# An attention block: earlier first tiles, projections released one by one, 280 instead of 252 VectorE score tiles, and another closing chain

## The chip, the cores and the metric

The kernel runs on one core of a Trainium2 chip. The metric is the time of one execution in microseconds of device time. Before the change it is 402.87 us, the median of three runs (402.79 to 403.15).

## The reference

One multi-head self-attention block in bfloat16: 2048 tokens (S), width 448 (D), 16 heads of 28 (Dh).

```python
B, S, D, H = 1, 2048, 448, 16          # x ~ 0.05 N(0,1), wqkv and wo too
qkv = (x @ wqkv).reshape(B, S, 3, H, Dh).transpose(2, 0, 3, 1, 4)
q, k, v = qkv[0], qkv[1], qkv[2]
scores = jnp.einsum("bhqd,bhkd->bhqk", q, k) * (Dh ** -0.5)
p = softmax(scores, axis=-1)
o = jnp.einsum("bhqk,bhkd->bhqd", p, v)
return o.transpose(0, 2, 1, 3).reshape(B, S, D) @ wo
```

## The kernel before

**Tiling.** Four heads make a group g (G = 4 groups), 512 queries make a chunk c (4 chunks). A *unit* u is one group with one chunk, so there are 16 units, worked through in the order u = 4g + c. In a unit the keys come in 16 blocks of 128 (kt), and each block gives four *tiles*, one per head: 128 keys by 512 queries of scores. There are 16 x 16 x 4 = 1024 tiles. TensorE makes the scores of a tile (matmul at L704), something turns them into exponentials, and TensorE multiplies these with V into one PSUM bank, ACC (L656), where all 16 key blocks of a unit add up. A column of ones in V gives the softmax sums in the same pass.

**Two ways to exponentials.** Most tiles go through ScalarE (L741): groups of three and two tiles in turn, each group one instruction, out to the slots of PT. The key blocks that `d_kts` names go through VectorE instead. For such a block (a *batch*, four tiles) VectorE first makes an integer from each score tile (L759, called R below, PSUM to PD), then three shifted copies of all four tiles (L766, called H, three instructions of 2048 elements). Read as bfloat16, these four rows of PD, each weighted by a copy of V that is scaled (VC, made by GpSimd at L465 from VX), add up to an approximated exponential. So a VectorE batch costs four passes of four PV matmuls where a ScalarE block costs one. Before, unit 0 has 3 batches and every other unit 4: 63 batches, 252 tiles; 772 tiles go to ScalarE.

**Projections.** `proj_qk` (L430) and `proj_v` (L450) make Q, K and V of one group and chunk, a *job* of 16 matmuls in one PSUM bank of the pool M (banks 5 and 6), which the scores of the VectorE tiles use too. VectorE copies a job's bank out (L410, L412, and VX at L459). Group 0's K and V stand at the front; the other 39 jobs carry priorities from L485.

**End of a unit.** `post_unit` copies ACC out (L593, ACCEV), sends the sums through DRAM and back in another layout (scr_l, LT), takes their reciprocal (L615), spreads it over partitions through DRAM (scr_r, RB), and GpSimd multiplies (L638) into OTN. When group 3 is done for a chunk, `out_proj` multiplies with wo (L570), VectorE copies (L582) and SyncE stores (L584). For the last unit the reciprocal goes through TensorE (L603, L625) and VectorE (L630) instead of DRAM. At the very end a flag says whether all reciprocals lie in a safe range (L780 to L790); every engine waits for it, and a slower general version would follow if it were 0.

**What sets the order.** The program is recorded first (`P.add` with engine, dependences, a planned duration `dur` and a priority) and then planned by `_Prog.schedule`: at each step the engine that can start first takes, among what is ready within 150 ns, the instruction with the lowest `prio`. The result is one fixed list per engine. The score matmuls have priorities about -1000, so they go as soon as their PSUM banks are free; projections fill in by priority.

**Loads.** SyncE loads x transposed, in four chunks (L349, L351), then wo (L385). ScalarE's queue loads wqkv in three parts K, Q, V of 448 columns (L357, L359). Nine rounds of four matmuls on zeros (L393) stand ahead of TensorE's first projection.

Of the kernel before, what the change touches and what calls it, by code (L numbers as in the profile page):

```python
# [7 lines left out]
ALU = mybir.AluOpType  # L8
# [251 lines left out]
NTERM = 4  # L260
ZBIAS = 127.0 * 128.0 - 7.235034912313908


def _fast(nc, x, wqkv, wo, out, n_heads=16):
# [16 lines left out]
    NPT = 30  # L281
    NZ = 3
    NOB = 4
    scale = float(DH) ** -0.5
# [12 lines left out]
    with es:  # L297
# [9 lines left out]
        VC = sb("VC", [128, NCH, NTERM, HC], BF16)  # L307
        VX = sb("VX", [128, 4, GD], FP32)
# [4 lines left out]
        OTN = sb("OTN", [128, G, S], BF16)  # L313
# [3 lines left out]
        SEL = sb("SEL", [128, 4], FP32)  # L317
        CK1 = sb("CK1", [128, NU * 16], FP32)
        CK2 = sb("CK2", [128, NU * 16], FP32)
        CKM = sb("CKM", [128, 1], BF16)  # L320
# [24 lines left out]
        dma_x = []  # L345
        for c in range(NCH):
# [6 lines left out]
        dma_w = {}  # L353
        wv_ = wqkv[0:(NIT - 1) * KT_, :].rearrange("(it p) c -> p it c", p=KT_)
        for t, prio in ((1, -20), (0, -19), (2, -18)):
            grp = _DmaGroup(f"w{t}")
            P.add("act", (lambda e, t=t: e.dma_start(w_raw[:, 0:NIT - 1, t * D:(t + 1) * D], wv_[:, :, t * D:(t + 1) * D])),  # L357
                  dur=600, prio=prio, name=f"dma_w{t}a", dma_group=grp, nbytes=(NIT - 1) * KT_ * D * 2)
            dma_w[t] = P.add("act", (lambda e, t=t: e.dma_start(w_raw[KT_ - KTAIL:KT_, NIT - 1, t * D:(t + 1) * D],  # L359
                                                                wqkv[(NIT - 1) * KT_:D, t * D:(t + 1) * D])),  # L360
                             dur=600, prio=prio + 0.5, name=f"dma_w{t}b", dma_group=grp, nbytes=KTAIL * D * 2)
# [6 lines left out]
                       deps=[id_f_op], dur=100, prio=-6, name="sel")  # L368
        V4 = V.rearrange("p n (hh r) -> p (n hh) r", r=32)
# [11 lines left out]
        for g in range(G):  # L381
            for h in range(4):
                r0 = (4 * g + h) * DH
                p0 = 32 * h
                dma_wo.append(P.add("sp", (lambda e, g=g, r0=r0, p0=p0: e.dma_start(wop[p0:p0 + DH, g, :], wo[r0:r0 + DH, :])),  # L385
                                    deps=[ms_wop], after=dma_wo[-1:] + dma_x[-1:], dur=500, prio=-5, name=f"dma_wo{g}{h}", dma_group=grp_wo))

        warm_last = None
        for i in range(9):
# [1124 lines left out]
```

## Time and profile before

| | |
|---|---|
| median of three runs | 402.87 us |
| the profiled execution's own time | 401.62 us |
| its span, first to last instruction | 398.0 us |
| mean granted TensorE clock | 0.927 |
| HBM read and written | 5.66 MB and 2.08 MB |

The page of the profile gives for each engine the time in which it was busy. The views used below are: the busy time by stretches of the span, groups of instructions by line, the timeline of one stretch, the table of waits, and the DMA queues. An instruction's duration in these views is from its start to its end; where instructions of one engine follow each other closely, the next starts a little ahead of the end of the last, so that the distance from start to start is shorter than the duration. That distance is called the *step* below.

### The profile page before, as it was taken

To read this page: it belongs to the slowest core of one execution; us is meant where nothing else is said; L and a number is where in the kernel's file an instruction comes from. 1 tells how busy PE (TensorE), PEld (TensorE's weight loads), DVE (VectorE), ACT (ScalarE), POOL (GpSimd) and SP (SyncE) were. 2 spreads that over 40 slices of the span, in tenths; PEclk is the share of its full clock that TensorE was granted. 3 is DMA by queue.
4 is the path that set the end of the run, shared out by engine and by line. 5 is a ranking of instruction groups with operands and counts; after the bars stand their busy time and mean duration, and the time that the engine had idled before them with its cause. 6 is when DMAs were issued, how large, how long until landed. Compare 5 with 4: busy or idle time off the path is not lost.

```text
span 398.0 us, 8639 instructions
## 1 busy us (share of the span) xinstructions
PE 348.9 (88%) x3713; PEld 106.6 (27%) x3713; DVE 334.0 (84%) x557; ACT 357.0 (90%) x314; POOL 48.5 (12%) x97
## 2 busy tenths in 40 slices
PE   4999999999999999999798887868887779889784
PEld 1333323323333233333221111211122112222141
DVE  0488999999999989999988788887788899999651
ACT  1599999999999999999999999999899999999811
POOL 6121121111112011312001010010101010010100
PEclk9899999999999999999968687898689999999886
DMA  9900010100000000101000000100001011001011
GB/s 216 133 12 2 12 37 1 32 0 24 8 17 16 4 28 3 29 1 31 2 16 15 3 27 3 29 0 18 13 4 29 2 29 36 19 23 51 26 49 53
DMA packets 20230, 10.47 MB, mean 26 GB/s; under 512 B 14364, under 2 KB 18204, under 8 KB 20184
## 3 DMA queue, kind: packets, MB, share of 16 engines
q1 hardware_dynamic: 18744, 8.64, 9.0%
q10 hardware_dynamic: 1440, 1.20, 1.2%
q8 instruction: 30, 0.49, 0.5%
q14 instruction: 16, 0.13, 0.1%
HBM read 5.66 MB, written 2.08 MB: 19 GB/s over the span
## 4 chain that ended last, share of the span: by engine, by line
PE 43%; DVE 28%; ACT 24%; DMA 2%; issue 1%; SPq 0%
ACT PT L741 24%; PE ps L656 16%; PE ps L704 16%; DVE PD L759 12%; DVE PD L766 11%; PE ps L430 6%; PE ps L570 2%; PE ps L450 2%; DVE OTS L593 2%; DMA xT<-in_x_dram 2%; DVE QT L410 1%; DVE KT L412 1%; DVE V L412 1%; SPq L349 0%; PE ps L625 0%
## 5 line engine op out<-in xcount | busy, mean ns | idle before, releaser
L741 ACT ACTIVATE PT<-ps 128x1536 bf16<-128x1536 f32 (+1 forms) x309 | 353.8, 1292 | 12.1 <-PE ps L704 10.9
L759 DVE TENSOR_SCALAR PD<-ps 128x512 int16<-128x512 f32 x252 | 169.5, 685 | 31.3 <-PE ps L704 29.9
L704 PE MATMUL ps<-QT,KT 28*128 28x512 bf16 x1024 | 148.2, 407 | 22.6 <-ACT PT L741 19.3
L766 DVE TENSOR_SCALAR PD<-PD 128x2048 int16<-128x2048 int16 x189 | 131.2, 713 | 0.9
L656 PE MATMUL ps<-PD,VC 128*32 128x512 bf16 x1008 | 98.6, 416 | 11.9 <-DVE PD L766 7.9
L656 PE MATMUL ps<-PT,V 128*32 128x512 bf16 x772 | 76.5, 408 | 1.1 <-DVE OTS L593 1.1
L704 PEld LDWEIGHTS ps<-QT,KT 28*128 28x128 bf16 x1024 | 36.0, 91 | 141.8 <-ACT PT L741 96.2
L638 POOL TENSOR_TENSOR OTN<-RB,OTS 128x512 bf16<-128x512 f32 x15 | 20.3, 1355 | 199.9 <-DMA RB<-scr_r 199.8
L430 PE MATMUL ps<-xT,w_raw 128*32 128x512 bf16 x512 | 40.7, 397 | 4.4 <-DMA xT<-in_x_dram 4.0
L656 PEld LDWEIGHTS ps<-PD,VC 128*32 128x32 bf16 x1008 | 24.7, 96 | 54.2 <-DVE PD L766 26.8
L465 POOL TENSOR_SCALAR VC<-VX 128x112 bf16<-128x112 f32 x64 | 21.9, 342 | 124.8 <-DVE VX L459 121.8
L656 PEld LDWEIGHTS ps<-PT,V 128*32 128x32 bf16 x772 | 18.4, 94 | 41.2 <-issue 36.4
L450 PE MATMUL ps<-w_raw,xT 128*128 128x112 bf16 x256 | 19.2, 214 | 0.5 <-DVE QT L410 0.5
L570 PE MATMUL ps<-wop,OTN 128*128 128x448 bf16 x64 | 18.1, 415 | 0.8 <-DVE OTN L630 0.8
L430 PEld LDWEIGHTS ps<-xT,w_raw 128*32 128x32 bf16 x512 | 11.8, 98 | 22.0 <-issue 10.3
L582 DVE CAST OUTS<-ps 128x448 bf16<-128x448 f32 x14 | 8.7, 621 | 8.8 <-PE ps L570 8.6
L412 DVE CAST KT<-ps 128x512 bf16<-128x512 f32 x16 | 11.0, 685 | 6.1 <-PE ps L430 6.0
L450 PEld LDWEIGHTS ps<-w_raw,xT 128*128 128x128 bf16 x256 | 13.2, 98 | 10.6 <-issue 7.6
L580 ACT ACTIVATE OUTS<-ps 128x448 bf16<-128x448 f32 x2 | 1.1, 543 | 12.7 <-PE ps L570 12.7
L593 DVE COPY OTS<-ps 128x512 f32<-128x512 f32 x16 | 11.0, 685 | 0.7 <-PE ps L656 0.7
L410 DVE TENSOR_SCALAR QT<-ps 128x512 bf16<-128x512 f32 x15 | 10.3, 685 | 1.0 <-PE ps L430 0.8
L412 DVE CAST V<-ps 128x448 bf16<-128x448 f32 x16 | 9.9, 617 | 1.1 <-PE ps L450 1.1
(37 smaller groups left out, 35.9 us busy)
## 6 DMA issues: line engine op xcount, KB each, us to landing
RB<-scr_r SPq DMA_DIRECT2D x60, 64.0 KB, 2.0
out_dram<-OUTS SPq DMA_DIRECT2D x16, 112.0 KB, 1.7
w_raw<-in_wqkv_dram ACTq DMA_DIRECT2D x3, 336.0 KB, 5.5
wop<-in_wo_dram SPq DMA_DIRECT2D x16, 24.5 KB
scr_l<-OTS SPq DMA_DIRECT2D x15, 8.0 KB
LT<-scr_l SPq DMA_DIRECT2D x15, 8.0 KB, 1.5
scr_r<-RS SPq DMA_DIRECT2D x15, 8.0 KB, 1.4
w_raw<-in_wqkv_dram ACTq DMA_DIRECT2D x3, 56.0 KB, 5.3
```

Of the source, the lines that this page charges most:

```text
L412: fe = (lambda e: e.tensor_copy(evac[0](), evac[1](hold[0].banks[0])))
L430: ins = e.matmul(ps[32 * h:32 * h + 32, b * 512:(b + 1) * 512], w_raw[:, it, col:col + 32], xT[:, it, c * 512:(c + 1) * 512], start=(it == ...
L450: ins = e.matmul(ps[:, b * 512 + j * GD:b * 512 + (j + 1) * GD], xT[:, it, n * 128:(n + 1) * 128], w_raw[:, it, 2 * D + g * GD:2 * D + (g ...
L465: sc = P.add("pool", (lambda e, dst=dst, j=j: e.tensor_scalar(dst, src, TERM_C[j], 1.0, ALU.mult, ALU.mult)), deps=[ev2, ms_c1[j]], after= ...
L570: return e.matmul(bank(hold[0].banks[0])[:, 0:D], OTN[:, gg, n * 128:(n + 1) * 128], wop[:, gg, :], start=(gg == 0), stop=(gg == G - 1))
L593: accev = P.add("dve", (lambda e: e.tensor_copy(OTS[:, ub, :], bank(ACC))), deps=pv_ops[u] + [ots_last[ub]], dur=610, prio=-95.0, name=f"A ...
L638: nm = P.add("pool", (lambda e: e.tensor_tensor(OTN[:, g, c * QCH:(c + 1) * QCH], RB[:, ub, :], OTS[:, ub, :], ALU.mult)), deps=[l4], dur= ...
L656: return e.matmul(ps[32 * h:32 * h + 32, ACC * 512:(ACC + 1) * 512], lhsT, rhs, start=first, stop=False, skip_group_check=True, tile_posit ...
L704: return e.matmul(bank(b), KT[32 * h:32 * h + DH, g, kt * 128:(kt + 1) * 128], QT[32 * h:32 * h + DH, g, c * QCH:(c + 1) * QCH], start=Tru ...
L741: ex = P.add("act", (lambda e, p0=p0, w=w, b0=b0: e.activation(PT[:, p0 * 512:(p0 + w) * 512], bank(b0, w), AF.Exp, scale=ESCALE)), deps=[ ...
L759: r = P.add("dve", (lambda e, hold=hold, zs=zs, h=h: e.tensor_scalar(PD[:, zs, 0, h * 512:(h + 1) * 512], bank(hold[0].banks[0]), ZBIAS, 0 ...
L766: sh = P.add("dve", (lambda e, zs=zs, j=j: e.tensor_scalar(PD[:, zs, j, :], PD[:, zs, 0, :], float(TERM_D[j]), None, ALU.add)), deps=rs_ + ...
```

## The change

- **Loads.** ScalarE's queue now loads only columns 0 to 115 of K, Q and V each (head group 0 and four columns more). The other 332 columns of all three go on SyncE's queue, behind all of x and ahead of wo.
- **Zero matmuls ahead of the first projection**: 14 rounds of four instead of 9. In addition `pv_common` can append rounds on zeros to a PV round, in a number that `warm_fill` decides after planning from the planned times: it appends one where the plan has a gap of more than 278 ns behind a PV round and counts less than 56% of the last 3413 ns as work.
- **Projections.** Priorities run from 0.8 in steps of 0.28 (before: 0.7 and 0.25), and the first matmul of each of these jobs may not stand ahead of the score group whose position is 0.06 before its priority.
- **VectorE tiles.** Units 3, 5, 7, 9, 11 and 13 get a fifth batch (key block 13), unit 0 a fourth: 70 batches, 280 tiles; 744 tiles are left to ScalarE, in 298 instructions instead of 309. Of the shifted copies, the first is one instruction as before (L862 of the changed kernel), the second and third are one of 4096 elements (L864). VC gets five slots instead of four, VX two blocks per job. PT has 36 slots instead of 30.
- **End of a unit.** The products go into QT, whose chunk is no longer needed, instead of OTN. The reciprocal of a unit has priority -96 instead of about u + 1.
- **Closing.** A new function `tail` takes the place of the last unit's chain: the last chunk's output projection for groups 0 to 2 is made ahead (PREOP); ACC is copied in two halves; one fp32 matmul with a 0/1 matrix (SELB) spreads the sums over the partitions; the reciprocal is taken of 128x256 values and multiplied, per half; then one matmul per output tile adds group 3 (FINOP). The range check of units 0 to 14 is made ahead, and of the last unit alone behind.

```diff
 def d_kts(u):
-    if u == 0:
-        return (3, 7, 15)
+    if u in (3, 5, 7, 9, 11, 13):
+        return (3, 7, 11, 13, 15)
     return (3, 7, 11, 15)
...
-    pr = 0.7 + i / 4.0
+    pr = 0.8 + i * 0.28
...
+    while release and release[0][0] - 0.06 <= pos:
+        release.pop(0)[1].after.append(s)
...
-for i in range(9):
+for i in range(14):
...
+wk = load_w("act", 0, 2, 0, GD + 4, "wqk0", -20)
+dma_w[(2, 0)] = load_w("act", 2, 3, 0, GD + 4, "wv0", -19)
 for c in range(NCH):                     # x, as before, on SyncE's queue
...
+wr = load_w("sp", 0, 3, GD + 4, D, "wr", -6.2)
...
-for j in range(1, NTERM):
-    sh = P.add("dve", (lambda e, zs=zs, j=j: e.tensor_scalar(PD[:, zs, j, :], PD[:, zs, 0, :], float(TERM_D[j]), None, ALU.add)), ...)
+h1 = P.add("dve", (lambda e, zs=zs: e.tensor_scalar(PD[:, zs, 1, :], PD[:, zs, 0, :], float(TERM_D[1]), None, ALU.add)), ...)
+h2 = P.add("dve", (lambda e, zs=zs: e.tensor_scalar(PD[:, zs, 2:4, :], PD[:, zs, 0:2, :], float(TERM_D[2]), None, ALU.add)), ...)
...
+def tail():
+    for j in range(NQT):                 # PREOP: groups 0 to 2 of the last chunk
+            for gg in range(G - 1):
+                ins = e.matmul(bank(j)[:, 0:D], QT[:, gg, n * 128:(n + 1) * 128], wop[:, gg, :], start=(gg == 0), stop=False, ...)
+    for k in range(2):                   # ACC copied in halves
+        av.append(P.add("dve", (lambda e, cs=cs: e.tensor_copy(OTS[:, ub, cs], bank(ACC)[:, cs])), ...))
+    for k in range(2):
+        bc = P.add("pe", (lambda e, ...: e.matmul(bank(...)[:, 0:H2], SELB[:, :], OTS[:, ub, cs], start=True, stop=True)), ...)
+        rc = P.add("dve", (lambda e, ...: e.reciprocal(RB[:, ub, cs], bank(...)[:, 0:H2])), ...)
+        dv = P.add("dve", (lambda e, ...: e.tensor_tensor(QT[...], OTS[:, ub, cs], RB[:, ub, cs], ALU.mult)), ...)
+        for j in (2 * k, 2 * k + 1):     # FINOP: group 3, then copy out and store
```

**Where the program differs: the start.** On ScalarE's queue, the loads of the weights w_raw stand first. Before:

```order
L357 DMA w_raw<-in_wqkv_dram 128x3x448
L359 DMA w_raw<-in_wqkv_dram 64x448
L357 DMA w_raw<-in_wqkv_dram 128x3x448
L359 DMA w_raw<-in_wqkv_dram 64x448
L357 DMA w_raw<-in_wqkv_dram 128x3x448
L359 DMA w_raw<-in_wqkv_dram 64x448
```

Of the change, ScalarE's queue up to the first activation that reads loaded data (the copy of Q):

```order
L383 DMA w_raw<-in_wqkv_dram 128x3x116 x2
L385 DMA w_raw<-in_wqkv_dram 64x2x116
L383 DMA w_raw<-in_wqkv_dram 128x3x116
L385 DMA w_raw<-in_wqkv_dram 64x116
L371 ACT_TABLE_LOAD
L371 ACTIVATE WARM<-WARM 128x1
L455 ACTIVATE QT<-ps 128x512
```

The three parts of 448 columns became three of 116; the remaining 3 x 332 columns stand on SyncE's queue behind the eight transposing loads of x.

**The middle.** TensorE's list before, where its last projection stands (L430; L704 are scores, L656 PV rounds): 497 of the 1024 score matmuls are ahead of it, which is in unit 7.

```order
L704 MATMUL ps<-QT,KT 128x512 x2
L430 MATMUL ps<-xT,w_raw 32x512 x4
L704 MATMUL ps<-QT,KT 128x512
L656 MATMUL ps<-PD,VC 32x512 x4
L704 MATMUL ps<-QT,KT 128x512 x4
L656 MATMUL ps<-PT,V 32x512 x8
```

TensorE's list of the change, where its last projection stands (L477; L798 are scores, L750 PV rounds): 920 score matmuls are ahead of it, which is in unit 14.

```order
L477 MATMUL ps<-xT,w_raw 32x512 x8
L798 MATMUL ps<-QT,KT 128x512 x2
L477 MATMUL ps<-xT,w_raw 32x512 x8
L750 MATMUL ps<-PD,VC 32x512 x4
L798 MATMUL ps<-QT,KT 128x512 x5
L750 MATMUL ps<-PD,VC 32x512 x4
```

The projections moved from units 0 to 7 (208, 64, 84, 76, 88, 76, 92 and 80 matmuls) to units 0 to 14 (160, 56, 56, 56, 52, 20, 80, 16, 64, 16, 48, 16, 112, 0 and 16). In the whole list of the change the only matmuls on zeros (ZM, ZW) are the 56 of the 14 rounds at the start: behind no PV round does one stand.

**The end.** TensorE's list before, from its last scores on (L570 is the output projection, 16 matmuls for a chunk; L603 and L625 turn and spread the reciprocal):

```order
L704 MATMUL ps<-QT,KT 128x512 x2
L570 MATMUL ps<-wop,OTN 128x448 x16
L656 MATMUL ps<-PT,V 32x512 x8
L603 MATMUL ps<-SEL,OTS 128x4 x4
L625 MATMUL ps<-id_f,RS 32x128 x16
L570 MATMUL ps<-wop,OTN 128x448 x16
```

TensorE's list of the change, from its last scores to the spreading of the sums (L620 is the output projection of the chunk before, L684 PREOP, L698 the spreading matmul):

```order
L798 MATMUL ps<-QT,KT 128x512
L620 MATMUL ps<-wop,QT 128x448 x8
L750 MATMUL ps<-PD,VC 32x512 x8
L750 MATMUL ps<-PT,V 32x512 x12
L750 MATMUL ps<-PD,VC 32x512 x8
L620 MATMUL ps<-wop,QT 128x448 x16
L750 MATMUL ps<-PD,VC 32x512 x8
L750 MATMUL ps<-PT,V 32x512 x12
L750 MATMUL ps<-PD,VC 32x512 x16
L684 MATMUL ps<-wop,QT 128x448 x3
L698 MATMUL ps<-OTS,SELB 128x256 x2
```

Behind the last scores there now stand 64 PV matmuls and 24 of the output projection instead of 8 and 16. Behind L698 follow the four matmuls for the range check (L724) and then, in turn, FINOP and the other three PREOPs.

More of the change, by code (lines that the diff above doesn't have):

```diff
@@ L280, in _fast @@
     GD = 4 * DH
-    NPT = 30
+    NPT = 36
     NZ = 3
     NOB = 4
+    NDK = len(D_SLOT)
     scale = float(DH) ** -0.5
@@ L569, in f_op @@
                 def f_op(e, gg=gg):
-                    return e.matmul(bank(hold[0].banks[0])[:, 0:D], OTN[:, gg, n * 128:(n + 1) * 128], wop[:, gg, :],
+                    return e.matmul(bank(hold[0].banks[0])[:, 0:D], QT[:, gg, n * 128:(n + 1) * 128], wop[:, gg, :],
                                     start=(gg == 0), stop=(gg == G - 1))
```

235 lines of the change are left out of this document (161 added, 74 removed).

## The prediction, made before the change was run

> **What bounds the kernel now.** First the page, for the engines' shares, then busy time by stretches, to see whether one engine holds the end everywhere.
>
> ```profile
> span 398.0 us, 8639 instructions
> ...
> PE 348.9 (88%) x3713; PEld 106.6 (27%) x3713; DVE 334.0 (84%) x557; ACT 357.0 (90%) x314; POOL 48.5 (12%) x97
> ```
>
> ```profile
> core 0: us, PE busy (x) PEld busy (x) DVE busy (x) ACT busy (x) POOL busy (x), PEclk, DMA share, GB/s
> 30.00:200.00 170.00, 163.68 (x1940) 54.05 (x1941) 164.01 (x280) 166.34 (x147) 27.93 (x59) 1.00 0.05 14
> 200.00:300.00 100.00, 82.81 (x765) 19.19 (x757) 80.84 (x131) 94.81 (x83) 5.22 (x4) 0.80 0.05 13
> 300.00:330.00 30.00, 22.97 (x245) 6.35 (x242) 26.02 (x42) 30.00 (x27) 2.91 (x2) 1.00 0.07 19
> 330.00:372.00 42.00, 38.31 (x374) 11.16 (x372) 39.16 (x66) 41.93 (x38) 1.49 (x1) 1.00 0.12 37
> ```
>
> ScalarE is busy 95 to 100% in every stretch, so from the first exponential to the last it is the bound. VectorE is as full (96.5%) only in 30:200, where the projections' copies are; afterwards it has 7 to 19% to spare. In 200:300 the granted clock is 0.80 and ScalarE loses 5.2 us of 100. So the change has room in the second half, and two ends to shorten.
>
> ```profile
> L741 ACT ACTIVATE PT<-ps 128x1536 bf16<-128x1536 f32 (+1 forms) x309 | 353.8, 1292 | 12.1 <-PE ps L704 10.9
> ```
>
> 353.8 us for 772 tiles are 0.458 us a tile. The 744 tiles left cost **341.0 us**, 12.8 less. Whether the time follows depends on VectorE, which takes the 28 tiles.
>
> **VectorE's sum.** Its steps, from start to start, stand in one full stretch of the timeline:
>
> ```profile
> 43.75 0.68 DVE L593 COPY OTS<-ps 128x512 f32<-128x512 f32 x1
> 44.35 2.47 DVE L759 TENSOR_SCALAR PD<-ps 128x512 int16<-128x512 f32 x4
> 46.74 0.68 DVE L766 TENSOR_SCALAR PD<-PD 128x2048 int16<-128x2048 int16 x1
> ...
> 51.00 0.24 DVE L615 RECIPROCAL RS<-LT 128x16 f32<-128x16 f32 x1
> 51.16 1.83 DVE L766 TENSOR_SCALAR PD<-PD 128x2048 int16<-128x2048 int16 x3
> 52.90 0.62 DVE L412 CAST V<-ps 128x448 bf16<-128x448 f32 x1
> 53.44 0.27 DVE L459 COPY VX<-ps 128x112 f32<-128x112 f32 x1
> 53.62 2.50 DVE L759 TENSOR_SCALAR PD<-ps 128x512 int16<-128x512 f32 x4
> ```
>
> ACCEV takes 0.60, four R 2.39 (0.60 each), three H 1.74 (taken as 0.60 each), the reciprocal 0.16, V 0.54, VX 0.18. From 512 and 448 columns (0.60, 0.54) the fixed part is about 0.12. No row shows H over 4096 elements: it costs at least 0.12 + 2 x 0.48 = 1.08 and at most two old steps, 1.20; I take 1.14. Also:
>
> ```profile
> L766 DVE TENSOR_SCALAR PD<-PD x189: 627/684/1767, 23.8 to 374.8; 128x2048 int16<-128x2048 int16 x189
> ```
>
> The median H is 684 ns, the page's mean 713: 189 x 0.029 = 5.5 us in which an H stretches, up to 1.77 us. I keep these 5.5.
>
> Up to the last H of the change: 280 R x 0.60 = 168.0; 70 first H x 0.60 = 42.0; 70 double H x 1.14 = 79.8; 31 copies of Q and K x 0.60 = 18.6; 16 V x 0.54 = 8.6; VX 12 x 0.18 + 4 x 0.29 = 3.3; 15 ACCEV x 0.60 = 9.0; 15 reciprocals x 0.16 = 2.4; 4 output copies x 0.54 = 2.2; stretching 5.5. Together **339.4 us**. The same list for before (252 R, 189 H) is about 316. So VectorE gains 23 us of work while ScalarE loses 13, and with 339 against 341 us the two are level. Neither is slack for the other any more. A full VectorE was busy 164.0 of 170 us in 30:200 beside a ScalarE at 98%; I take that share, 0.965: 339.4 / 0.965 = **351.7 us**. At 0.94 it would be 361, at 0.985 345. ScalarE alone, at its 98% of that stretch, would need 348.
>
> **The start.**
>
> ```profile
> 1.18 4.03 PE L393 MATMUL ps<-ZM,ZW 128*32 128x512 bf16 x36 [1.18 <-POOL ZM L340]
> ...
> 9.24 4.29 PE L430 MATMUL ps<-xT,w_raw 128*32 128x512 bf16 x48 [4.03 <-DMA xT<-in_x_dram]
> ...
> 12.72 0.60 ACT L408 ACTIVATE QT<-ps 128x512 bf16<-128x512 f32 x1 [6.99 <-PE ps L430]
> ...
> 13.90 4.62 ACT L741 ACTIVATE PT<-ps 128x1536 bf16<-128x1536 f32 x4 [0.58 <-PE ps L704]
> ```
>
> ```profile
> q1 hardware_dynamic: 18744, 8.64, 9.0%
> q10 hardware_dynamic: 1440, 1.20, 1.2%
> ```
>
> The first projection waits for x (landed at 9.2), K and Q take to 12.7, the first exponential starts at 13.90. The rows of the two queues give packets, megabytes and share. On the way x (SyncE's queue, q1) shares the DMA engines with 1.20 MB of weights (q10): 1440 packets in 1.2% of 16 x 398 us are 76 us of engine time, 4.8 us for all 16. Now 896 packets (232 bytes each) are ahead or beside, 448 follow. At 30.6 ns (queue q1's mean: 9.0% over 18744) to 53 ns a packet, the 896 are 1.7 to 3.0 us. So x lands 1.8 to 3.1 us earlier; I take **7.0** instead of 9.2. Nothing (9.2) is the other end. K and Q took 3.4 us at half pace:
>
> ```profile
> 9.00:10.00 1.00, 0.76 (x8) 0.29 (x12) 0.00 (x0) 0.00 (x0) 0.00 (x0) 0.50 1.28 287
> ...
> 13.00:14.00 1.00, 1.00 (x18) 0.15 (x10) 0.41 (x1) 0.42 (x2) 0.00 (x0) 1.00 1.07 224
> ```
>
> The clock stood at 0.50 there and came back about 3 us later. Fourteen zero rounds at the pace of the nine (4.03 / 9 = 0.45) last to 7.4, up to the arrival, so I take a mix, 2.4 us, between 1.7 and 3.4. The first exponential is then at 7.0 + 2.4 + the same 1.2 behind = **10.6**, 3.3 earlier (bounds 0 and 4.8). The weights of groups 1 to 3 come behind x and are first read in unit 1; there I cost them nothing, and if that cover were gone unit 1 would wait.
>
> On packet size the Trainium skill (DMA: Bandwidth & Descriptors, Why small descriptors are slow and Specifications) speaks against this edit: transfers under 512 bytes miss line rate, and 232 is under it. The two queues' rows cannot settle it, since no row isolates packets of 232 bytes; by that rule the later end, a landing near 9.2, is the nearer one and the sum would be 2.2 us more.
>
> **The end.**
>
> ```profile
> 378.17 1.02 ACT L741 ACTIVATE PT<-ps 128x1024 bf16<-128x1024 f32 x1 [0.23 <-PE ps L704]
> ...
> 378.06 4.77 PE L570 MATMUL ps<-wop,OTN 128*128 128x448 bf16 x16
> ...
> 382.76 0.61 PE L656 MATMUL ps<-PT,V 128*32 128x512 bf16 x8
> ...
> 384.18 1.05 PE L603 MATMUL ps<-SEL,OTS 128*128 128x4 f32 x8 [0.80 <-DVE OTS L593]
> 385.27 0.26 DVE L608 RECIPROCAL RS<-ps 128x16 f32<-128x16 f32 x1 [1.15 <-PE ps L603]
> ...
> 386.73 0.69 DVE L630 TENSOR_TENSOR OTN<-ps,OTS 128x512 bf16<-128x512 f32 x1 [0.41 <-PE ps L625]
> ...
> 392.40 0.54 ACT L580 ACTIVATE OUTS<-ps 128x448 bf16<-128x448 f32 x1 [1.48 <-PE ps L570]
> ```
>
> Before, the last PV ends at 383.4, the last copy to OUTS at 392.9, the span at 398.0: 9.5 and 5.1 us. The store and the flag behind stay: **5.1**.
>
> Of the change, the last H ends at 10.6 + 351.7 = 362.3; the last scores stand one R and two H earlier, 2.4 us, at 359.9. Behind them are 24 output matmuls (4.77 / 16 = 0.30 each, 7.2 us) and 16 PV rounds at 0.22 (3.5): **10.7**, and 15.8 if all runs at half pace (0.37 and 0.43); 8 at full pace. So the last PV ends at 370.6.
>
> Then: two half copies to +0.8 (0.69 for 512 columns gives 0.42 and a step of 0.33); the spreading matmul about 0.6; two rounds of reciprocal and product. The reciprocal of 256 columns is in no row: 16 columns take 0.26, which with one column a cycle more gives about 0.5, while a slope like that from nothing to 16 would give 1.7. I take 0.5, nearer to the 0.69 of the product over 512; at the other end the close is 2.4 longer. The second product ends at +3.0. Meanwhile TensorE must do, in its order, the range check's four matmuls (1.05), FINOP, six PREOP matmuls, two FINOPs, three PREOPs and the last FINOP: some 13 x 0.30 + 1.05 = 5.0 behind the spreading at +1.5, so the last one is at +6.1 and its copy at **+6.7** (5.9 at full pace, 8 at half), 2.8 less than 9.5. TensorE, not the shorter chain, sets this.
>
> **The clock.** The title's zero passes behind PV are not in the program: planning found no place for one. So nothing holds the clock in the second half but the projections that moved there.
>
> ```profile
> PE ps L704 <- ACT PT L741: 19.3, 49, 1.0
> ```
>
> TensorE's longest wait for ScalarE was 1.0 us, yet the clock was 0.80 in 200:300, from where the projections ended. The odd units 5 to 15 now have one job or none. ScalarE lost 5.2% at that clock; for 6 units of 22 us at a quarter of it I add **1.7 us** (bounds 0 and 6.9).
>
> The Trainium skill (TensorE: Matmul & The Clock Gate, Why this matters for your kernels) says the clock drops only behind idle gaps of about 3 us. The row above disagrees: waits of 1.0 us and a clock of 0.80 stand together. By that rule the 1.7 us fall away.
>
> **The sum.** 10.6 + 351.7 - 2.4 + 10.7 + 6.7 + 5.1 + 1.7 = 384.1 us of span against 398.0, so -13.9. The profiled execution, 401.62, would be 387.7; its median beside it is 402.87, so I forecast **389.0 us**. Part by part: start -3.3, closing -2.8, the rest in the middle.
>
> **Rivals.**
> - *VectorE hides better, or the close runs at full pace.* For it: in 30:200 it was ScalarE that was full, VectorE may do more. At 0.985 the middle is 7 us shorter, the close 2 to 3: about 380. Against: only two PSUM banks serve R and the projections.
> - *Lockstep.* Units with five batches cost VectorE 5 x (2.40 + 0.60 + 1.14) = 20.7, + 0.8 for ACCEV and reciprocal + one job's copies 0.6 + stretching 0.4 = 22.5, over 0.965 = 23.3 us; units with four cost ScalarE 48 x 0.458 = 22.0, over 0.978 = 22.5. If PT's 36 slots cannot carry a lead from one unit to the next, 6 x 23.3 + 10 x 22.5 = 364.8 instead of 351.7: 402, **no change**. Against: the lag is about 2 us a unit, four tiles of 36.
> - *The clock, slower than before.* If it drops already with 46 projection matmuls a unit where before there were about 80, all units from 1 to 12 run at half pace for part of the time. A unit without jobs took 22.0 / 0.948 = 23.2 us there; 3.6 jobs at 1.4 us (4.29 / 3) are 5.1 more, less TensorE's idle 17% of 23.2, 4.0, and the extra PV rounds of odd units 0.6 (three at 0.43, every other unit): 24.9, against 22.0, times 12 is +35 us: 424. It turns slower from +14, that is from a clock that is low in about 40% of these units. Against: at 1.00 in 300:330 with no projections at all.
> - *The start stays* (x still lands at 9.2): 392.
>
> **Chances.** Forecast (384 to 396) 0.62; better hidden 0.15; lockstep 0.14, of which 0.08 still faster, 0.04 the same; the clock 0.07; start unchanged 0.02. That is faster by over 0.2% (about the least that can be told from no change) 0.87, same 0.04, slower 0.09. The range reaches from the second case to lockstep: 379 to 402.
>
> **What would show it.** Start: first exponential near 10.6. Middle: VectorE busy 96% or more in every stretch of 30:340, ScalarE about 95%; VectorE waiting for TensorE's scores in the odd units speaks for lockstep. L864 at a step of 1.14. Granted clock above 0.9 up to unit 12. End: 10.7 us from the last scores to the last PV, 6.7 to the last copy. I am wrong if VectorE shows more than 5% idle, or if a double H costs more than 1.2.

## The result, and the profile after

| | before | changed |
|---|---|---|
| median of four runs | 402.83 us | 396.46 us |
| lowest and highest | 401.88, 403.15 | 392.81, 401.31 |
| profiled execution, span | 401.62, 398.0 us | 393.24, 391.4 us |
| mean granted TensorE clock of the profiled execution | 0.927 | 0.964 |

The ratio of changed to before is **0.976** (95% interval 0.9731 to 0.979): faster, as forecast, and 7.5 us slower than the 389.0 that was forecast. The whole range of the forecast, 379 to 402, holds; its main part, 384 to 396 with a chance of 0.62, ends just below the median. Two of the four runs of the changed kernel (399.68 and 401.31) were executions with a lower granted clock (0.943 and 0.94), and the comparisons leave such runs out.

The page of the changed kernel: span, shares of the engines, the chain that ended last, and the costliest groups (busy, mean ns, idle time before and its releaser).

```profile
span 391.4 us, 8768 instructions
...
PE 364.3 (93%) x3789; PEld 113.4 (29%) x3789; DVE 360.1 (92%) x544; ACT 346.8 (89%) x303; POOL 54.6 (14%) x97
...
PE 48%; DVE 45%; ACT 2%; issue 2%; DMA 1%; SPq 0%
...
L838 ACT ACTIVATE PT<-ps 128x1536 bf16<-128x1536 f32 (+1 forms) x298 | 343.7, 1248 | 18.6 <-PE ps L798 16.9
...
L798 PE MATMUL ps<-QT,KT 28*128 28x512 bf16 x1024 | 172.4, 395 | 9.6 <-DVE PD L856 2.9
...
L864 DVE TENSOR_SCALAR PD<-PD 128x4096 int16<-128x4096 int16 x70 | 88.9, 1277 | 0.1
L798 PEld LDWEIGHTS ps<-QT,KT 28*128 28x128 bf16 x1024 | 42.0, 91 | 144.9 <-DVE PD L856 50.2
```

ScalarE's exponentials fell from 353.8 to 343.7 us (341.0 was reckoned), but its idle time ahead of them rose from 12.1 to 18.6 us. ScalarE has all but left the chain (2%, before 24%). The weight loads ahead of TensorE's scores now wait mostly for VectorE's R: 50.2 us at L798 against 10.7 before. This is no idle time of TensorE as such, since other matmuls run on beside most of it: the score matmuls themselves wait 2.9 us for R, 0.8 before. The stretches that were shown of before, in the same view (the column behind POOL's is the granted clock, 1.00 is full speed):

```profile
30.00:200.00 170.00, 159.91 (x1700) 48.31 (x1703) 163.04 (x243) 159.55 (x139) 22.02 (x37) 0.94 0.06 14
200.00:300.00 100.00, 97.16 (x1040) 30.08 (x1040) 98.88 (x151) 98.03 (x86) 15.53 (x25) 1.00 0.06 16
300.00:330.00 30.00, 27.81 (x286) 7.65 (x287) 29.55 (x42) 27.18 (x24) 2.53 (x2) 1.00 0.04 11
330.00:372.00 42.00, 40.55 (x338) 11.05 (x330) 39.16 (x60) 39.36 (x35) 2.53 (x2) 0.92 0.10 28
```

In 200:300, where before the clock was 0.80, it is 1.00 and ScalarE, VectorE and TensorE are all at 97 to 99%. In 30:200 the clock is 0.94 and ScalarE at 94%, before 98%. ScalarE gains 3.2 us in 200:300 and loses 6.8 in 30:200 and 5.4 in 300:372.

Cut at four marks, the profiled executions of this and of some kernels below read as follows. The columns are the start of the first exponential, the start of the last score matmuls, the end of the last PV round, the end of the last copy to OUTS and the end of the span, in us; the middle is the second less the first.

| kernel | first exp. | last scores | middle | last PV | last copy | span |
|---|---|---|---|---|---|---|
| before (252 tiles) | 13.90 | 377.52 | 363.6 | 383.37 | 392.94 | 398.0 |
| changed (280) | 9.98 | 370.11 | 360.1 | 379.07 | 386.75 | 391.4 |
| changed with 252 tiles | 10.06 | 363.63 | 353.6 | 367.15 | 374.83 | 379.3 |
| 252, projections as before | 10.21 | 372.79 | 362.6 | 376.31 | 385.06 | 389.4 |
| 252, start as before | 13.80 | 368.29 | 354.5 | 371.81 | 379.49 | 384.2 |
| 280, VectorE lighter | 9.98 | 361.9 | 351.9 | 370.89 | 378.57 | 383.5 |

From before to the changed kernel that is -3.9 at the start, -3.5 in the middle, +3.1 from the last scores to the last PV, -1.9 in the close and -0.4 behind it, together -6.6.

### The profile page after: what moved, and what is told of

It reads as the page before. It is cut to its first block, busy times and chain, and to the rows that moved or that the text cites. A ratio compares the mean times of both kernels' runs of the same rounds, so it can differ in the third digit from the quotient of the medians.

```text
span 391.4 us, 8768 instructions
## 1 busy us (share of the span) xinstructions
PE 364.3 (93%) x3789; PEld 113.4 (29%) x3789; DVE 360.1 (92%) x544; ACT 346.8 (89%) x303; POOL 54.6 (14%) x97
## 4 chain that ended last, share of the span: by engine, by line
PE 48%; DVE 45%; ACT 2%; issue 2%; DMA 1%; SPq 0%
DVE PD L856 21%; PE ps L798 20%; PE ps L750 18%; DVE PD L864 11%; DVE PD L862 6%; PE ps L477 4%; PE ps L620 2%; DVE OTS L648 2%; PE ps L499 2%; ACT PT L838 2%; DVE QT L457 2%; DVE KT L459 1%; DMA xT<-in_x_dram 1%; DVE RB L701 1%; DVE V L459 1%
## 5 line engine op out<-in xcount | busy, mean ns | idle before, releaser
L838 ACT ACTIVATE PT<-ps 128x1536 bf16<-128x1536 f32 (+1 forms) x298 | 343.7, 1248 | 18.6 <-PE ps L798 16.9
L856 DVE TENSOR_SCALAR PD<-ps 128x512 int16<-128x512 f32 x280 | 180.1, 681 | 10.2 <-PE ps L798 6.5
L798 PE MATMUL ps<-QT,KT 28*128 28x512 bf16 x1024 | 172.4, 395 | 9.6 <-DVE PD L856 2.9
L750 PE MATMUL ps<-PD,VC 128*32 128x512 bf16 x1120 | 99.2, 397 | 3.6 <-DVE PD L864 2.6
L864 DVE TENSOR_SCALAR PD<-PD 128x4096 int16<-128x4096 int16 x70 | 88.9, 1277 | 0.1
L798 PEld LDWEIGHTS ps<-QT,KT 28*128 28x128 bf16 x1024 | 42.0, 91 | 144.9 <-DVE PD L856 50.2
L750 PE MATMUL ps<-PT,V 128*32 128x512 bf16 x744 | 69.6, 402 | 3.5 <-DVE OTS L648 3.5
L862 DVE TENSOR_SCALAR PD<-PD 128x2048 int16<-128x2048 int16 x70 | 49.6, 727 | 0.1
L662 POOL TENSOR_TENSOR QT<-RB,OTS 128x512 bf16<-128x512 f32 x15 | 20.8, 1384 | 191.6 <-DMA RB<-scr_r 191.5
L515 POOL TENSOR_SCALAR VC<-VX 128x112 bf16<-128x112 f32 (+1 forms) x64 | 27.0, 422 | 124.7 <-DVE VX L508 121.6
L477 PE MATMUL ps<-xT,w_raw 128*32 128x512 bf16 x512 | 38.5, 383 | 1.6 <-DMA xT<-in_x_dram 0.9
L750 PEld LDWEIGHTS ps<-PD,VC 128*32 128x32 bf16 x1120 | 25.1, 95 | 49.1 <-issue 34.2
L750 PEld LDWEIGHTS ps<-PT,V 128*32 128x32 bf16 x744 | 17.4, 95 | 36.0 <-issue 25.5
L477 PEld LDWEIGHTS ps<-xT,w_raw 128*32 128x32 bf16 x512 | 10.6, 95 | 18.2 <-issue 8.2
L712 ACT ACTIVATE OUTS<-ps 128x448 bf16<-128x448 f32 x2 | 1.1, 544 | 12.8 <-PE ps L709 12.8
L648 DVE COPY OTS<-ps 128x512 f32<-128x512 f32 x15 | 10.3, 685 | 1.5 <-PE ps L750 1.3
L620 PE MATMUL ps<-wop,QT 128*128 128x448 bf16 x48 | 11.3, 355 | 0.1
```

What stands on the lines that cost most here:

```text
L477: ins = e.matmul(ps[32 * h:32 * h + 32, b * 512:(b + 1) * 512], w_raw[:, it, col:col + 32], xT[:, it, c * 512:(c + 1) * 512], start=(it == ...
L515: sc = P.add("pool", (lambda e, dst=dst, j=j: e.tensor_scalar(dst, src, TERM_C[j], 1.0, ALU.mult, ALU.mult)), deps=[ev2, ms_c1[j]], after= ...
L620: return e.matmul(bank(hold[0].banks[0])[:, 0:D], QT[:, gg, n * 128:(n + 1) * 128], wop[:, gg, :], start=(gg == 0), stop=(gg == G - 1))
L662: nm = P.add("pool", (lambda e: e.tensor_tensor(QT[:, g, c * QCH:(c + 1) * QCH], RB[:, ub, :], OTS[:, ub, :], ALU.mult)), deps=[l4], dur=1 ...
L750: return e.matmul(ps[32 * h:32 * h + 32, ACC * 512:(ACC + 1) * 512], lhsT, rhs, start=first, stop=False, skip_group_check=True, tile_posit ...
L798: return e.matmul(bank(b), KT[32 * h:32 * h + DH, g, kt * 128:(kt + 1) * 128], QT[32 * h:32 * h + DH, g, c * QCH:(c + 1) * QCH], start=Tru ...
```

## The experiments

Each experiment ran beside the kernel before, in three rounds in which that had medians of 400.83, 403.83 and 403.06 us. The ratios are to the kernel before of the same round, and they are what is compared between rounds.

**Zero rounds behind PV.** A round of four matmuls on zeros (L735) behind every second PV round of seven units, 101 in all, to see whether that keeps the clock up.

```diff
-warm_fill(P, fillable, pv_ops)
+last_u = {u: max(ops, key=lambda o: o.t0) for u, ops in pv_ops.items()}
+for u in (5, 7, 9, 11, 13, 14, 15):
+    rounds = sorted(((op, f) for op, f, v in fillable if v == u), key=lambda t: t[0].t0)
+    for k, (op, f) in enumerate(rounds):
+        if k % 2 == 1 and op is not last_u[u]:
+            f.fill = 1
```

> The changed kernel with 101 rounds of four zero matmuls that really stand in the program, behind every second PV round of units 5, 7, 9, 11, 13, 14 and 15 (the units with few projections). Theory A (the granted clock): in the changed kernel's trace the clock stands at 0.50 in four stretches, together about 32 us, three of them in units 5, 7 and 14, and both VectorE and ScalarE lose some 2 us in each. Then the dips of units 5, 7 and 14 go, the mean granted clock rises from 0.964 to about 0.98, and the span falls from 391.4 by 5 to 7 us, to 384 to 386. Theory B (VectorE is simply full, its list is longer than 351.7 us by itself): the span stays at 391 or grows, since the zero rounds only add work to TensorE.

Measured: 416.09 us (411.17 to 420.07), ratio 1.0406 (1.0348 to 1.0465), slower than before. The groups of this kernel:

```profile
L838 ACT ACTIVATE PT<-ps 128x1536 bf16<-128x1536 f32 (+1 forms) x298 | 346.9, 1242 | 32.0 <-PE ps L798 29.9
...
L735 PE MATMUL ps<-ZM,ZW 128*32 128x512 bf16 x404 | 40.3, 389 | 0.0
```

The zeros took 40.3 us of an engine that was 93% busy, ScalarE waited 32.0 instead of 18.6 us, and the clock was 0.956, no better. Theory A falls. Zero rounds in this number and these places are no remedy; nothing here suggests that the change lost anything by not getting them.

**252 tiles.** The changed kernel with the tiles of before.

```diff
-            if u in (3, 5, 7, 9, 11, 13):
-                return (3, 7, 11, 13, 15)
+            if u == 0:
+                return (3, 7, 15)
```

> The changed kernel with the 252 VectorE tiles of before (unit 0 three batches, every other unit four), all else as changed. Theory A and the prediction (the tiles are worth having): ScalarE gets 772 x 0.458 = 353.6 us, over 0.98 = 361, from a first exponential at 10.0 to about 371 to 374, and the span is 390 to 394, the same as with 280 or up to 3 us more. Theory C (the 28 tiles cost as much as they give, or more, because VectorE becomes the bound and its stalls lower the clock): the span is 386 to 389, shorter than with 280.

Measured: 382.81 us (381.01 to 383.91), ratio **0.9543** (0.9499 to 0.9586) against 0.976 with 280. The 28 tiles, which the forecast counted as 12.8 us less work for ScalarE, cost 2.2%. The groups and two stretches of this kernel:

```profile
L838 ACT ACTIVATE PT<-ps 128x1536 bf16<-128x1536 f32 (+1 forms) x309 | 351.6, 1314 | 4.0 <-PE ps L798 3.0
...
L798 PE MATMUL ps<-QT,KT 28*128 28x512 bf16 x1024 | 141.8, 395 | 25.8 <-ACT PT L838 22.3
```

```profile
30.00:200.00 170.00, 153.66 (x1834) 48.51 (x1831) 161.35 (x243) 169.52 (x151) 23.57 (x39) 1.00 0.06 16
200.00:300.00 100.00, 87.80 (x948) 24.73 (x945) 89.96 (x132) 98.25 (x87) 11.61 (x21) 0.92 0.05 14
```

ScalarE has 7.9 us more to do and 14.6 less idle time. It is the bound again (169.52 of 170), with VectorE at 95% and TensorE at 90%. The same 1024 score matmuls, each as long as before (395 ns), keep TensorE busy 141.8 us here and 172.4 with 280 tiles: there, fewer of them run side by side. The forecast counted only the extra PV rounds for TensorE. Planning anew also lets `warm_fill` find a place for a few zero rounds behind PV rounds: one here, two with 268 tiles, four with 252 tiles and the projections as before, seven with 236. A round kept TensorE busy for 0.40 us in the run above (40.3 us for 101), so these few do not explain the differences.

**Projections as before, with 280 tiles.**

```diff
-            pr = 0.8 + i * 0.28
+            pr = 0.7 + i / 4.0
...
-            while release and release[0][0] - 0.06 <= pos:
-                release.pop(0)[1].after.append(s)
```

> The changed kernel with the projections' priorities of before and without the release behind score groups. The list puts the last projection at 925 of 1024 score matmuls, as the change (920), so the release moves little. If the release matters by itself (theory D), the span changes by more than 3 us and the dips of the clock move; otherwise it stays within 2 us of 391.4.

Measured: 394.52 us (386.93 to 414.77), ratio 0.9686 (0.9612 to 0.976). It overlaps with the changed kernel's, so nothing can be told. With 280 tiles the plan puts the last projection late either way, at the 925th of 1024 score matmuls here and at the 920th in the changed kernel, so this run tests little. The release of the projections by itself stays untested.

**The close.** The reciprocal of 128x16 values first, then 16 small matmuls that spread it (32 instructions in the profile), instead of spreading first and taking two reciprocals of 128x256.

```diff
-                rc = P.add("dve", (lambda e, ...: e.reciprocal(RB[:, ub, cs], bank(...)[:, 0:H2])), ...)
+            rs = P.add("dve", (lambda e: e.reciprocal(RS[:, us], bank(N1B)[:, 0:16])), ...)
...
+                        ins = e.matmul(ps[...], RS[:, i:i + 1].to_broadcast([128, 32]), id_f[:, :], start=True, stop=True, ...)
```

> The changed kernel with the closing chain in another order: the reciprocal is taken of 128x16 sums and spread over the partitions afterwards (as the kernel before did), the output projection of groups 0 to 2 stays ahead. In the changed kernel's trace the two reciprocals of 128x256 take 1.75 us each. Theory E (these two set the close): from the last PV to the last copy it takes 7.7 us there, and here 0.8 + 1.1 + 0.3 + 1.1 + 0.8 + waits 0.5 + the last matmul and copy 1.5 = 6.1, so the span falls by about 1.5. The prediction's step (TensorE's order sets the close) expects no change, since TensorE's matmuls are the same or more.

Measured: 397.87 us, ratio 0.9783 (0.9698 to 0.9867): with 280 tiles the runs scatter from 390 to 412, and the time says nothing. In the trace, though, the last PV ends at 397.56 and the last copy at 403.48: 5.9 us against 7.7. With 252 tiles it could be measured (below).

**VectorE made lighter.** The list of every engine is unchanged; from the fourth batch on, the double H writes one row instead of two.

```diff
-h2 = P.add("dve", (lambda e, zs=zs: e.tensor_scalar(PD[:, zs, 2:4, :], PD[:, zs, 0:2, :], float(TERM_D[2]), ...
+h2 = P.add("dve", (lambda e, zs=zs, j3=(4 if bi < NZ else 3): e.tensor_scalar(PD[:, zs, 2:j3, :], PD[:, zs, 0:j3 - 2, :], float(TERM_D[2]), ...
```

> The changed kernel with the same instructions in the same order on every engine; only from the fourth batch on the third of the shared values of the double H is written alone (128x2048 as L862, about 0.7 us) and the fourth keeps what an earlier batch left, so part of the output is not computed. VectorE loses 67 x (1.28 - 0.71), about 38 us, and 360.1 busy becomes about 322; TensorE and ScalarE have the same work. Theory C (28 more VectorE tiles filled VectorE; TensorE waits with its scores for it, its clock dips, and ScalarE is starved): ScalarE is the bound again, its idle time falls from 18.6 us to 7 or less, the last scores come from 370 to 358 - 361 and the time goes from 393 to 379 - 384, with all runs within 3 us of each other. Rival P (TensorE, 364.3 us busy with the extra PV rounds and the spread projections, is itself the bound): the time stays at 388 - 396, the clock still dips, ScalarE stays idle behind TensorE.

Measured: 387.19 us (384.78 to 394.94), ratio 0.9595 (0.9533 to 0.9657). The chain and groups of this kernel:

```profile
PE 61%; ACT 23%; DVE 13%; issue 1%; POOL 0%; POOLq 0%
...
L838 ACT ACTIVATE PT<-ps 128x1536 bf16<-128x1536 f32 (+1 forms) x298 | 341.7, 1271 | 12.4 <-PE ps L798 11.0
```

The last scores came from 370.1 to 361.9, with the lists unchanged, so VectorE's fullness made a large part of the middle's loss. It did not do so by way of the clock, which is 0.963 here and 0.964 in the changed kernel. But the size was missed: 358 to 361 was expected, ScalarE still idles 12.4 us (7 or less was expected), and the time is 3 us above the expected range. With VectorE out of the way TensorE holds the chain (61%), and the way from the last scores to the last PV stays at 9.0 us. In the table the middle is only 1.7 us shorter than with 252 tiles, though ScalarE has 9.9 us less to do (341.7 against 351.6). The weight loads of the scores still wait 41.5 us for R, so most of the 50.2 us above lies in the order of the list and not in VectorE's load. This speaks for 280 tiles being too many for TensorE's list as well.

**268 tiles**: a fifth batch in units 5, 9 and 13 alone.

> 67 batches, 268 VectorE tiles (a fifth batch in units 5, 9 and 13 alone); all else as the changed kernel. With 252 tiles the time was 382.8 us and VectorE 334.0 busy, with 280 about 393 to 400 and 360.1. Theory C (loss sets in where VectorE's list comes level with ScalarE's): VectorE about 349, ScalarE about 346, so the level is just reached: ScalarE idle 5 - 12 us, time 381 - 388. Rival Q (each fifth batch costs by itself, 10.4 to 14 us over seven batches = 1.5 - 2 us each): 382.8 + 4 x 1.75 = 389 - 391, even in steps. By the forecast's own rule (each tile moved is worth 0.458 us): 382.8 - 16 x 0.458 = 375.5.

Measured: 387.7 us (385.5 to 390.22), ratio 0.9625 (0.9575 to 0.9675). In ratios, the four batches from 252 to 268 cost 0.2% each, the three to 280 0.45% each; the intervals are as wide as that difference, so an onset and even steps cannot be told apart. The forecast's own rule (375.5) is out.

**252 tiles, projections as before**: the old priorities and no release.

> 252 tiles, and the projections at the priorities of before, none released (they end in unit 7 instead of unit 11). Theory S (spreading the projections keeps TensorE busy and its clock up in the later units): as in the kernel before, the clock falls in 200:300 (0.80 there, 0.92 with 252 tiles and the spread), ScalarE loses 3.4 us more in that stretch (94.81 busy against 98.25), time 386 - 388. Rival N (with 252 tiles ScalarE has what it needs either way): within 1.5 us of 382.8.

Measured: 389.72 us (386.37 to 392.82) beside a before of 403.83, ratio 0.9646 (0.9589 to 0.9703), above the interval of 252 tiles alone. The step in the ratios, 1.0%, is 4 us; 3.2 to 5.2 were expected. The stretch that was at stake:

```profile
200.00:300.00 100.00, 82.50 (x762) 18.84 (x762) 80.56 (x111) 93.70 (x83) 6.34 (x5) 0.80 0.06 15
```

The clock is 0.80 as before the change, ScalarE at 93.70 (98.25 with the spread). Spreading the projections over units 0 to 11 instead of 0 to 7 is worth those 4 us (9 us in the middles of these two profiled executions; this one is among the longer runs of its kernel).

**252 tiles, start as before**: the old weight loads and 9 zero rounds.

> 252 tiles, and the weight loads of before (q, k and v whole on the ScalarE queue, no small load first, 9 zero rounds instead of 14). The start is worth what the first exponential moved: 13.90 before, 10.06 with 252 tiles and the small loads. Theory (the gain of the start is carried to the end): first exponential near 13.9, time 382.8 + 3.5 to 4 = 386 - 387. Rival (what is lost ahead of the first exponential is won back, since the second head group's weights then come earlier): within 1.5 us of 382.8.

Measured: 387.68 us (385.31 to 392.1), ratio 0.9621 (0.9569 to 0.9674), 0.8% or 3 us above 252 tiles. The intervals overlap a little, but the marks in the table are clear: the first exponential is 3.7 us later, the last scores 4.7 and the last copy 4.7. What the start gains is carried to the end.

**TensorE made lighter.** The lists are unchanged again; the fourth PV round of a batch covers 32 columns instead of 512.

```diff
+                    hh, n = 4 * g + h, (32 if j == 3 and (u, h) in opened else 512)
...
-                                PD[:, zs, j, h * 512:(h + 1) * 512].bitcast(BF16))
+                                PD[:, zs, j, h * 512:h * 512 + n].bitcast(BF16), n)
```

> The changed kernel with the same instructions in the same order on every engine; only the fourth PV round of a batch covers 32 columns instead of 512 (the rest of that partial product is left out of the output). TensorE loses about 70 rounds x 0.4 us = 28 us of 364 busy; VectorE (360 us) and ScalarE keep their work. With VectorE made lighter by 38 us (the run before) the last scores came from 370.1 to 361.9 us and TensorE still ran 8.5 us behind them. Theory C (VectorE's list alone holds the middle; TensorE's extra rounds only make the tail): last scores stay at 366 - 371, the way from them to the last PV falls from 9.0 to 3 - 5: time 0.962 - 0.972 of before. Rival T (TensorE's load holds the middle as much as VectorE's, either relief is enough): last scores at 358 - 363, tail 3 - 5, time 0.94 - 0.955 of before.

Measured: 419.1 us (416.76 to 432.55), ratio 1.0474 (1.0409 to 1.0539). Both theories fall: the span is 27 us longer than that of the changed kernel, and the last scores start at 397.4. The row of the granted clock in 40 slices, and the groups:

```profile
PEclk9999999999995588765579997599999655659998
...
L838 ACT ACTIVATE PT<-ps 128x1536 bf16<-128x1536 f32 (+1 forms) x298 | 346.4, 1251 | 43.3 <-PE ps L798 40.9
...
L798 PE MATMUL ps<-QT,KT 28*128 28x512 bf16 x1024 | 188.7, 438 | 12.0 <-ACT PT L838 3.5
```

With less work TensorE was given less clock: 0.846 over the span instead of 0.964. A score matmul took 438 ns instead of 395, and ScalarE waited 43.3 us. So a shorter PV list is no gain as such, and TensorE's speed is not a constant of this kernel. Why the clock fell is open; with it, this run cannot tell what TensorE's load alone costs.

**236 tiles**: three batches in units 0, 3, 6, 9 and 12.

> 59 batches, 236 VectorE tiles (three instead of four batches in units 0, 3, 6, 9 and 12); all else as the changed kernel. If ScalarE is the bound at 252 tiles (351.6 busy, 4.0 idle), 16 tiles more on it cost 16 x 0.458 = 7.3 us: 382.8 + 7.3 = 390, 0.972 of before. Rival (VectorE or TensorE still hold 252 tiles back, the best number is lower): 382.8 + 3 or less, 0.962 of before or below.

Measured: 398.57 us (393.31 to 400.92), ratio 0.9932 (0.9846 to 1.0017). ScalarE's work grew by 8.1 us (359.7 busy; 7.3 expected), but its idle time also, from 4.0 to 12.1 us, at a clock of 0.937. The loss is larger than ScalarE's work on this side too, and this rise of the idle time is not explained. Of the four counts tried, 252 is the best.

**252 tiles with the other close.**

> 252 tiles and the closing chain with the reciprocal of 128x16 ahead of the spreading matmul, in place of two reciprocals of 128x256 at 1.75 us. The chain was 5.9 us from the last PV to the last copy in the run with 280 tiles, against 7.7: 1.8 us less, 382.8 - 1.8 = 381, 0.950 of before. Rival (TensorE's products behind the chain set the close, not VectorE): 382.8, 0.9543 of before; the way from last PV to last copy stays above 7.

Measured: **378.98 us** (377.75 to 380.23), ratio 0.9485 (0.9436 to 0.9533), the fastest of all, 0.6% under 252 tiles alone with overlapping intervals. VectorE's timeline from the last PV (which ends at 364.98) on:

```profile
365.04 0.76 DVE L692 COPY OTS<-ps 128x256 f32<-128x256 f32 x2 [0.58 <-PE ps L755]
367.06 0.26 DVE L702 RECIPROCAL RS<-ps 128x16 f32<-128x16 f32 x1 [1.26 <-PE ps L699]
...
368.68 0.76 DVE L717 TENSOR_TENSOR QT<-ps,OTS 128x256 bf16<-128x256 f32 x2 [0.74 <-PE ps L710]
369.76 1.16 DVE L729 CAST OUTS<-ps 128x448 bf16<-128x448 f32 x2 [0.32 <-PE ps L723]
```

From the last PV to the last copy are 5.9 us instead of 7.7.

**252 tiles, three single H.**

```diff
-h2 = P.add("dve", (lambda e, zs=zs: e.tensor_scalar(PD[:, zs, 2:4, :], PD[:, zs, 0:2, :], float(TERM_D[2]), ...
+for j in range(1, NTERM):
+    sh = P.add("dve", (lambda e, zs=zs, j=j: e.tensor_scalar(PD[:, zs, j, :], PD[:, zs, 0, :], float(TERM_D[j]), ...
```

> 252 tiles and three single H of 128x2048 per batch as before, instead of one and a double one. The double H ran 1.24 us, two single ones 2 x 0.715 = 1.43: VectorE gets 63 x 0.19 = 12 us more busy, of 334. Theory (252 tiles leave VectorE slack): within 2 us of 382.8, 0.954 +- 0.005 of before. Rival (VectorE is close enough to full that 12 us bring back part of the loss of the 280 tiles): 387 - 391, 0.965 - 0.975.

Measured: 386.79 us (381.96 to 388.15), ratio 0.965 (0.9575 to 0.9725). VectorE's busy time grew by 6.5 us in the H (129.7 against 78.2 + 45.0), half of what was expected. The ratio lies at the rival's lower end and its interval overlaps with that of 252 tiles, so the double H is probably, but not surely, worth some 4 us.

## Why the prediction was right, and where it was off

The direction and the range held, but the mechanism of the middle did not: the tiles that were to bring most of the gain cost 2.2%. The gain comes from other parts: the start (3 us) and the spread projections (4 us), both measured with 252 tiles, the close (1.9 us in the table) and probably the double H (some 4 us). With a gain of 9.7 us by the ratio where 13.9 were forecast, the range held in part by luck. The sum of the span was 384.1 and the span 391.4; the terms were off by -0.6 (start), +9.1 (middle with the clock), -1.7, +1.0 and -0.4.

**The start: right.** x landed at 6.9 us (7.0 forecast) and the first exponential began at 9.98 (10.6):

```profile
6.93 1.91 PE L477 MATMUL ps<-xT,w_raw 128*32 128x512 bf16 x32 [0.90 <-DMA xT<-in_x_dram]
...
9.98 1.45 ACT L838 ACTIVATE PT<-ps 128x1536 bf16<-128x1536 f32 x1 [0.49 <-PE ps L798]
```

Q and K ran at a granted clock of 1.00 (1.91 us for 32 matmuls), near the lower bound. The landing speaks against the later end by the Trainium skill (DMA: Bandwidth & Descriptors, Why small descriptors are slow): packets of 232 bytes did not hold x back here.

**The middle: the step that failed.** "So VectorE gains 23 us of work while ScalarE loses 13 ... I take that share, 0.965: 339.4 / 0.965 = 351.7 us." The list was right within 2 us. A double H steps at 1.13 us, 1.14 forecast. The stretching is the mean less the median of both H, whose minimum, median and maximum stand in the view by line:

```profile
L864 DVE TENSOR_SCALAR PD<-PD x70: 1161/1217/2287, 20.2 to 368.3; 128x4096 int16<-128x4096 int16 x70
```

That is 70 x (1277 - 1217) + 70 x (727 - 683) ns = 7.3 instead of 5.5 us (the second pair is L862's). The share was not: from the first exponential to the end of the last H (369.48) are 359.5 us, and 341.2 of them make 0.949. And the last scores, forecast 2.4 us ahead of the last H, came 0.6 behind it: they waited for ScalarE, whose list ended later than VectorE's. One place of what the share left out stands in the following rows of the timeline of the changed kernel.

```profile
51.33 0.39 PE L798 MATMUL ps<-QT,KT 28*128 28x512 bf16 x4
51.40 1.26 POOL L662 TENSOR_TENSOR QT<-RB,OTS 128x512 bf16<-128x512 f32 x1 [19.81 <-DMA RB<-scr_r]
51.46 2.29 DVE L864 TENSOR_SCALAR PD<-PD 128x4096 int16<-128x4096 int16 x1
...
53.67 0.68 DVE L856 TENSOR_SCALAR PD<-ps 128x512 int16<-128x512 f32 x1
...
54.40 0.60 PE L798 MATMUL ps<-QT,KT 28*128 28x512 bf16 x4 [1.36 <-DVE PD L856]
...
55.05 2.37 ACT L838 ACTIVATE PT<-ps 128x1536 bf16<-128x1536 f32 x2 [0.81 <-PE ps L798]
```

GpSimd's product starts 0.06 us ahead of a double H, which takes 2.29 us instead of 1.22. R stands behind it, a PSUM bank comes free late, TensorE's list stops for 1.36 us at the score that needs it, and ScalarE, whose scores stand behind, idles. The same matmuls then take 0.60 instead of 0.39. Busy times of the same place in steps of 2 us:

```profile
52.00:54.00 2.00, 1.04 (x15) 0.56 (x12) 2.00 (x2) 2.00 (x2) 0.66 (x1) 1.00 0.05 12
54.00:56.00 2.00, 1.60 (x12) 0.42 (x12) 1.97 (x5) 1.19 (x2) 0.73 (x3) 0.94 0.00 0
56.00:58.00 2.00, 2.00 (x17) 0.41 (x16) 1.47 (x3) 1.41 (x2) 0.41 (x2) 0.50 0.00 0
58.00:60.00 2.00, 2.00 (x26) 0.57 (x26) 1.86 (x3) 1.70 (x2) 0.00 (x0) 0.71 0.00 0
```

The clock stands at 0.50 for 3.4 us (0.24 us in 54:56, all of 56:58, 1.16 in 58:60), with TensorE busy all the time (2.00), and VectorE, which was full, now waits too (1.47). ScalarE loses 1.7 us in the six from 54 on. So here a stall of 1 us in one full engine is followed by a half-speed stretch in which all three lose time. The changed kernel has four stretches at 0.50 ahead of its last scores (from about 56, 127, 172 and 336 us). A product of GpSimd stands 4 to 12 us ahead of each, but behind ten others of the fifteen no such stretch follows, so that the stretched H makes the clock fall is not shown. Nor is the low clock by itself what sets 280 tiles apart: over the span it is 0.964 with 280 tiles, 0.963 with the lighter H and 0.969 with 252 tiles, while ScalarE's idle time is 18.6, 12.4 and 4.0 us. What differs is what such a stretch costs. Ten us of the changed kernel and ten of the kernel with 252 tiles, both at a low clock:

```profile
130.00:140.00 10.00, 9.74 (x80) 2.11 (x76) 7.60 (x12) 7.50 (x7) 0.00 (x0) 0.62 0.02 2
290.00:300.00 10.00, 9.37 (x67) 1.76 (x63) 7.42 (x11) 9.80 (x9) 0.00 (x0) 0.53 0.00 0
```

With 280 tiles (the upper row) ScalarE loses 2.5 us, with 252 tiles 0.2 at a lower clock still. In slices of 10 us from 10 on, those with a clock under 1.00 hold 10.3 of the 18.1 us that ScalarE idles up to 370 in the changed kernel, and 8.9 of the 11.9 up to 360 with the lighter H. So VectorE's relief took most of the idle time at full clock (7.8 to 3.0 us) and little of the rest.

That VectorE's fullness is a cause of the middle's loss is shown by the lighter H (-8.2 us in the middle, equal lists); fewer tiles (-6.5) agree, but they change TensorE's list too. An estimate of its share: with 7.9 us less of exponentials than with 252 tiles (343.7 against 351.6) the middle should have been 353.6 - 7.9 = 345.7 instead of 360.1, and of these 14.4 us the lighter H, which takes VectorE below its load with 252 tiles (325.6 against 334.0 us busy), wins 8.2 back. The rest stays open between TensorE's longer list and what a low clock costs it. What makes the clock drop is not settled. TensorE's waits come ahead of it at the place above, cutting TensorE's work made it worse, and adding zeros did not help. The Trainium skill (TensorE: Matmul & The Clock Gate, What's actually happening) has the clock fall after an idle window of about 3.4 us; the longest idle time in the rows above is 1.36 us, so this rule by itself does not describe these traces. The prediction had noted that and still priced the clock at 1.7 us.

**The end: count right, pace and bound off.** The 24 output matmuls and 16 PV rounds behind the last scores took 9.0 us (10.7 forecast, 8 "at full pace"). They are themselves a price of the 280 tiles: with 252 tiles 9 and 5 stand there, 3.5 us. The close took 7.7 instead of 6.7. Some 0.4 of that is a slip in the sum: by its own terms TensorE is done at 1.5 + 5.0 = 6.5, and a copy of 0.6 behind it ends at 7.1. The mechanism was wrong through a term taken at the wrong end: "I take 0.5" for the reciprocal of 256 columns, which is 1.75 us, twice (one column in a cycle was assumed; the rows give 6.2 ns a column):

```profile
380.33 1.76 DVE L701 RECIPROCAL RB<-ps 128x256 f32<-128x256 f32 x1 [0.46 <-PE ps L698]
382.12 0.42 DVE L703 TENSOR_TENSOR QT<-OTS,RB 128x256 bf16<-128x256 f32 x1
382.47 1.75 DVE L701 RECIPROCAL RB<-ps 128x256 f32<-128x256 f32 x1
384.25 0.43 DVE L703 TENSOR_TENSOR QT<-OTS,RB 128x256 bf16<-128x256 f32 x1
```

So VectorE sets the close, and not TensorE, which the prediction had named. TensorE waits for L703 twice (1.09 and 0.44 us).

**The rivals.** "VectorE hides better" fell. "Lockstep" fell as a mechanism: VectorE's waits for scores went down, not up (6.5 us from TensorE's scores at L856, 29.9 before); the waiting runs the other way. "The clock, slower than before" was right that the clock takes part, wrong in place and size: it fell in four stretches, not in all units with few projections. The test "wrong if VectorE shows more than 5% idle" gave 4.1% in 30:200, 1.1% in 200:300 and 6.8% in 330:372, most of which lies behind the 340 up to which VectorE was to be full. "The start stays" fell with the landing at 6.9 us. That the zero passes behind PV "are not in the program" was right.

## What to carry to other kernels

Moving work from the bound engine to one that then becomes level with it is not worth the difference of the two lists: leave the second engine slack (VectorE was busy 334 us of 379 with 252 tiles; with 268, at 347 of 386, the loss had probably begun), and count what the move adds to the third (TensorE's scores and PV rounds here). Where the granted clock changes within a run, as here, ask which engine has slack to cover a slow stretch, and try the count on both sides, as 236, 252, 268 and 280 were here. Before a short chain at the end is made shorter, put a price on its slowest instruction: a reciprocal belongs on the smallest shape (16 columns), ahead of the spreading.

## What the runs showed of the hardware that was not expected

- VectorE's reciprocal of 128x256 fp32 values from PSUM took 1.75 us, of 128x16 0.25 to 0.26 us: 1.50 us for 240 columns, 6.2 ns a column, where the product beside it took 0.42 us for 256.
- A double H that began 0.06 us behind a product of GpSimd took 2.29 us instead of the median 1.22: 1.07 more, where the product still had 1.20 us to run. The Trainium skill (SBUF — State Buffer, SBUF: two separate sides) describes an exclusive lock of a port pair that VectorE and GpSimd share, held for a whole instruction; the rows at 51.40 and 51.46 agree with it.
- The granted clock fell with less work on TensorE and equal lists: 0.964 to 0.846 when one PV round in four of the batches shrank to 32 columns. Ten us at a low clock cost ScalarE 2.5 us with 280 tiles (clock 0.62) and 0.2 us with 252 (clock 0.53).
